# Scores two groups ahead of use, the gate in front of the squares on VectorE, and v's first loads behind z

## The chip, the cores and the metric

One core of one Trainium2 chip. The time is what the device takes for one execution, in microseconds (us). The kernel before takes 1231.67 us, the median of the 3 runs that the prediction could see (1231.24 to 1232.58). The experiments compare kernels in rounds on one chip: a ratio is the mean time of one kernel's fast runs over the mean time of the other kernel's fast runs of the same rounds, so it is not quite the ratio of the medians that stand beside it. The changed kernel was run in one round only, so an experiment is compared with it through the two ratios to the kernel before. A trace is of one run, and not always of a typical one.

In the lines of the profile, PE is TensorE's matmuls and PEld its weight loads, DVE is VectorE, ACT ScalarE, POOL GpSimd and SP SyncE; a q behind a name means the engine's queue. L282 is line 282 of the kernel in question, and the same statement has other line numbers in other kernels.

## The reference, cut to what matters

```python
# u, v: (8, 3008, 256)   z: (8, 3008, 64)   all float32
scores = (1.0 / S) * np.matmul(z, z.transpose(0, 2, 1))
attn = np.maximum(scores, 0.0) ** 2
x = u * np.matmul(attn, v)                       # the gate is this product with u
xt = x.transpose(0, 2, 1)
h = np.maximum(xt @ w_tok1, 0.0) @ w_tok2        # w_tok1 3008x256, w_tok2 256x3008
u2 = x + h.transpose(0, 2, 1)
out = u2 + np.maximum(u2 @ w_ch1, 0.0) @ w_ch2   # w_ch1 256x1536, w_ch2 1536x256
```

## The kernel before

A batch is cut into 6 blocks of 512 queries and 6 blocks of 512 keys, so it has 36 *groups* (a query block with a key block); groups are numbered n = 0 to 287 over the 8 batches. A group makes scores (TensorE), relu (ScalarE), squares (VectorE) and then 8 products with v (TensorE), 4 into each of two accumulators, one for each half of the 256 channels. In the last key block, two of the 8 (the *tail products*, one for each accumulator) have only 64 rows and come first. (The recorded texts say "block" for group where they speak of scores one or two blocks ahead.) At the end of a query block the *gate* multiplies both accumulators by u and so frees them for the next block. From batch 1 on, a squared block above the diagonal is also turned by a DMA transpose (a *flip*), which saves its mirror image, and the matmuls of the mixer of the batch before are strewn between the groups. Batch 0 has no mixer work and no flips.

```python
def scores(b, q, g):
    ...                                       # 4 matmuls (L229) into two tiles sc (tag "ps", bufs=3)
    at = sb.tile(..., tag="at", bufs=3)
    for pr, sc in enumerate(pss):
        rl = sb.tile(..., tag="rl", bufs=3)
        nc.scalar.activation(rl, sc, ACT.Relu, scale=inv_S)             # L242
        nc.vector.tensor_mul(at pair, rl, rl)                           # L246 if flipped, else L248
    if flip:
        nc.sync.dma_start_transpose(out=fl, in_=at[:])                  # L252

def gate(b, q, dh):
    nc.vector.tensor_mul(xT[:, dh], acc[dh], uT[:, :, dh])              # L308 (L313: the ragged rest)
    if dh == DT - 1:
        nc.sync.dma_start_transpose(out=x, in_=xT)                      # L317, x_sb for the mixer

def load_u(b, q): nc.gpsimd.dma_start(out=ur, in_=u rows)               # L145
def turn_u(b, q): nc.sync.dma_start_transpose(out=uT, in_=ur)           # L154

def load_w_tok2(c):                           # six parts, once per kernel
    st = sb.tile(..., tag="ws", bufs=1)       # one staging buffer
    nc.gpsimd.dma_start(out=st, in_=w_tok2 part c)                      # L171
    for h in range(DT):
        nc.gpsimd.tensor_copy(w_tok2_sb part, st)                       # L175

# what is asked for at which group (fetch[n] is issued at the head of group n)
at_group(base + q * NG + 2, lambda m=m: load_u(m // NQ, m % NQ))        # m: two blocks on
at_group(base + q * NG + 5, lambda m=m: turn_u(m // NQ, m % NQ))
at_group(base + (NQ - 1) * NG - 2 + (j if j > 1 else 0),
         lambda b=b, c=c: load_v(b + 1, c))                             # v of the next batch
at_group(NG + 1 + 4 * c, lambda c=c: load_w_tok1(c))
at_group(NG + 3 + 4 * c, lambda c=c: load_w_tok2(c))                    # groups 9, 13, ..., 29
at_group(2 * NG + 6 * part, lambda part=part: load_w_ch(part))

for n, (b, q, g) in enumerate(groups):
    for f in fetch.get(n, []): f()
    if n + 2 < NG: turn_first_z(zr0[vorder[n + 2]], zTs[0], vorder[n + 2])
    if direct_block(b, q, g): scores(*directs[ahead]); ahead += 1       # ahead starts at 1
    ...
    if not last:
        half(0); mix(n, got / 2); half(1); mix(n, 0.0)                  # half: 4 products, L282
    else:
        half(0); gate(b, q, 0); half(1); gate(b, q, 1); mix(n, 0.0)
```

`turn_first_z` turns a block of batch 0's z with four small matmuls and a copy out of PSUM by ScalarE; `double_z` makes the doubled bf16 copy that it turns; `fill(n)` issues n matmuls on zeros, to keep TensorE busy while the first data come.

## Time and profile before

| | before |
|---|---|
| time | 1231.67 us |
| span of the profiled run | 1230.7 us |
| TensorE (PE) busy | 97% |
| VectorE, ScalarE, GpSimd busy | 49%, 41%, 12% |
| waits of PE for gate, first squares, flipped squares | 12.1, 4.6, 2.0 us |

TensorE is the bound, so only what makes it start later counts. The lines that say so are in the prediction. GpSimd asks for u, v, the weights and, from batch 1 on, z.

### The profile page before, as it was taken

What the parts mean: (1) busy time and instruction counts of PE and PEld (TensorE: products, weight loads), DVE (VectorE), ACT (ScalarE), POOL (GpSimd) and SP (SyncE); (2) the same over time, 40 slices, a digit from 0 to 9 for tenths busy, and PEclk for the clock granted to TensorE, in tenths of its full rate; (3) what the DMA queues carried; (4) which work ended last, traced back from release to release, by engine and by line L of the source; (5) the groups of instructions that cost most, each with busy time, mean ns of one, the idle gap of its engine ahead of it and who ended that gap; (6) DMA issues with size and microseconds to landing.
All of it is one profiled execution on the core that took longest, in us unless ns stands there. A gap on an engine that the chain in (4) does not pass through costs nothing.

```text
span 1230.7 us, 17401 instructions
## 1 busy us (share of the span) xinstructions
PE 1198.9 (97%) x7105; PEld 626.3 (51%) x7105; DVE 603.6 (49%) x781; ACT 503.1 (41%) x525; POOL 142.5 (12%) x271
## 2 busy tenths in 40 slices
PE   7999999999999999999999999999999999999998
PEld 2334445554555445564455545455455554555566
DVE  3665654436553464435544355544544436553443
ACT  5776444343533434324434244433444334442122
POOL 2442010100101001111011111011010110000000
PEclk8999999999999999999999999999999999999999
DMA  7999966897767967669677787678866797653122
GB/s 132 147 120 146 155 134 124 136 150 134 124 140 130 159 111 141 144 116 166 118 144 131 123 145 123 131 148 129 151 122 129 132 151 129 128 106 83 33 78 67
DMA packets 436223, 157.20 MB, mean 128 GB/s; under 512 B 400112, under 2 KB 413744, under 8 KB 436144
## 3 DMA queue, kind: packets, MB, share of 16 engines
q1 hardware_dynamic: 408800, 123.78, 52.4%
q0 software_dynamic: 27344, 32.32, 19.7%
q8 instruction: 55, 0.90, 0.3%
q14 instruction: 24, 0.20, 0.0%
HBM read 65.40 MB, written 24.64 MB: 73 GB/s over the span
## 4 chain that ended last, share of the span: by engine, by line
PE 85%; DVE 7%; issue 3%; ACT 3%; DMA 1%; SPq 0%; DVEq 0%; ACTq 0%
PE acc L282 36%; PE op L389 20%; PE hp L371 18%; PE sc L229 6%; PE a_ps L336 3%; DVE xT L354 3%; ACT rl L242 2%; DVE h2pre L376 1%; DVE xT L308 1%; DVE at L248 1%; DVE at L246 1%; DMA fl<-at 1%; DMA zf<-in_z_dram 1%; PE h_ps L350 1%; ACT h2pre L378 1%
## 5 line engine op out<-in xcount | busy, mean ns | idle before, releaser
L242 ACT ACTIVATE rl<-sc 128x1024 bf16<-128x1024 f32 (+1 forms) x366 | 352.1, 1014 | 378.2 <-PE sc L229 373.0
L282 PE MATMUL acc<-at,v_sb 128*128 128x512 bf16 (+3 forms) x1464 | 359.7, 379 | 19.8 <-DVE xT L308 12.1
L282 PEld LDWEIGHTS <-v_sb 128*128 128x128 bf16 (+1 forms) x2304 | 207.8, 98 | 296.5 <-issue 100.2
L389 PE MATMUL op<-w_ch_sb,h2pre 128*128 128x256 bf16 (+1 forms) x2304 | 279.1, 273 | 0.8
L371 PE MATMUL hp<-xT,w_ch_sb 128*128 128x512 bf16 (+1 forms) x1152 | 274.8, 374 | 1.3 <-DVE xT L354 0.2
L378 ACT ACTIVATE h2pre<-hp 128x1024 bf16<-128x1024 f32 (+1 forms) x144 | 144.8, 1005 | 281.7 <-PE hp L371 280.9
L389 PEld LDWEIGHTS <-h2pre 128*128 128x128 bf16 (+1 forms) x2304 | 224.3, 98 | 62.1 <-ACT h2pre L378 6.3
L246 DVE TENSOR_TENSOR at<-rl 128x1024 bf16<-128x1024 bf16 x210 | 145.7, 695 | 191.3 <-ACT rl L242 187.7
L376 DVE TENSOR_SCALAR h2pre<-hp 128x1024 bf16<-128x1024 f32 (+1 forms) x144 | 172.5, 1199 | 78.8 <-PE hp L371 78.7
L282 PE MATMUL acc<-fl,v_sb 128*128 128x512 bf16 (+1 forms) x840 | 200.3, 370 | 0.0
L371 PEld LDWEIGHTS <-w_ch_sb 128*128 128x128 bf16 x1152 | 112.6, 98 | 131.4 <-issue 4.4
L248 DVE TENSOR_TENSOR at<-rl 128x1024 bf16<-128x1024 bf16 (+1 forms) x156 | 108.2, 702 | 94.5 <-ACT rl L242 94.3
L397 DVE TENSOR_TENSOR res<-op,u_sb 128x512 f32<-128x512 f32 x88 | 60.5, 688 | 155.7 <-PE op L389 155.7
L229 PE MATMUL sc<-zT 64*128 64x512 bf16 (+1 forms) x732 | 113.0, 381 | 2.0 <-DVE xT L354 1.0
L308 DVE TENSOR_TENSOR xT<-acc,uT 128x512 bf16<-128x512 f32 (+1 forms) x96 | 61.5, 663 | 62.8 <-PE acc L282 62.4
L145 POOL DMA_DIRECT2D ur<-in_u_dram x48 | 26.0, 542 | 434.8 <-DMA uT<-ur 434.2
L354 DVE TENSOR_TENSOR xT<-xT,h_ps 128x1024 bf16<-128x1024 bf16 (+1 forms) x48 | 53.9, 1191 | 23.0 <-PE h_ps L350 23.0
L96 POOL COPY zr<-zs 128x512 bf16<-128x512 bf16 x42 | 27.7, 660 | 311.9 <-DMA zT<-zr 311.5
L229 PEld LDWEIGHTS <-zT 64*128 64x128 bf16 x732 | 22.1, 94 | 70.6 <-issue 69.7
L350 PE MATMUL h_ps<-w_tok_sb,a_sb 128*128 128x512 bf16 (+1 forms) x192 | 43.3, 374 | 1.6 <-ACT a_sb L342 0.7
L336 PE MATMUL a_ps<-x_sb,w_tok_sb 128*128 128x256 bf16 x384 | 44.4, 273 | 0.0
L135 POOL DMA_DIRECT2D v_sb<-in_v_dram x48 | 26.0, 548 | 135.7 <-PE acc L282 135.6
(33 smaller groups left out, 157.1 us busy)
## 6 DMA issues: line engine op xcount, KB each, us to landing
out_dram<-res SPq DMA_DIRECT2D x88, 256.0 KB, 2.3
v_sb<-in_v_dram POOLq DMA_DIRECT2D x40, 256.0 KB, 4.1
ur<-in_u_dram POOLq DMA_DIRECT2D x40, 256.0 KB, 4.9
zs<-in_z_dram POOLq DMA_DIRECT2D x35, 64.0 KB, 4.9
fl<-at SPq DMA_TRANSPOSE x105, 4.4
v_sb<-in_v_dram POOLq DMA_DIRECT2D x8, 192.0 KB, 5.0
w_ch_sb<-in_moe_w_ch_dram POOLq DMA_DIRECT2D x4, 384.0 KB, 6.0
ur<-in_u_dram POOLq DMA_DIRECT2D x8, 192.0 KB, 5.6
```

Source lines behind the costliest of these rows:

```text
L229: nc.tensor.matmul(sc[:, r, :W], zT[h, k * P:(k + 1) * P], zT[h, q * QW:q * QW + W], start=True, stop=True)
L242: nc.scalar.activation(rl[:, :, :W], sc[:, :, :W], ACT.Relu, scale=inv_S)
L246: nc.vector.tensor_mul(a4[:, :, pair, :], r4, r4)
L248: nc.vector.tensor_mul(a3[:, pair, :W], rl[:, :, :W], rl[:, :, :W])
L282: nc.tensor.matmul(o, vt[rows, i, dh * P:(dh + 1) * P], rhs, start=st, stop=sp, skip_group_check=True)
L308: nc.vector.tensor_mul(xT[:, dh, :full * P].rearrange("p (t s) -> p t s", s=P), acc[:, :full * P].rearrange("p (t s) -> p t s", s=P), uT[: ...
L336: nc.tensor.matmul(st["a_ps"][:, th, :], w_tok1_sb[:, k, th * P:(th + 1) * P], x[:, :, i, :], start=(k == 0 and th == 0), stop=(k == KT - ...
L354: nc.vector.tensor_add(xT[:, :, :W], xT[:, :, :W], h[:, :, :W])
L371: nc.tensor.matmul(hp[:, r, :W], w_ch1_sb[:, dc, cc * P:(cc + 1) * P], xT[:, dc, :W], start=(dc == 0), stop=(dc == DT - 1))
L376: nc.vector.tensor_single_scalar(h2[:, :, :W], hp[:, :, :W], 0.0, AX.max)
L378: nc.scalar.activation(h2[:, :, :W], hp[:, :, :W], ACT.Relu)
L389: nc.tensor.matmul(op[:rows[i], i, :], st["h2", q, cc // 2][:, cc % 2, c0:c0 + rows[i]], w_ch2_sb[:, cc, :], start=(cc == 0 and i == 0), s ...
```

## The change

The intent is to take away three kinds of stall of TensorE: at the start (all z doublings were in front of the first squares), at block ends (the squares of the next group were in front of the gate), and in later batches (squares ready too late). Scores are made two groups ahead, so that their squares can be issued behind the gate; the first z blocks no longer share the DMA with all of v.

```diff
-    for pr, sc in enumerate(pss):            # in scores(): relu, square, relu, square
+    for sc in pss:                           # relu, relu; the squares are handed back
         rl = sb.tile(...); nc.scalar.activation(rl, sc, ACT.Relu, scale=inv_S)
-        ... squares of this pair
+        rls.append(rl)
+    def squares(): ...                       # squares, and the flip
+    return squares
 ... # start
-    for c in vorder: load_v(0, c)
+    zr0 = [double_z(zf0[c], nc.vector) for c in range(DT)]
+    for c in range(NG):
+        if DT <= c: zr0.append(double_z(zf0[c], nc.gpsimd))
+        load_v(0, c)                         # behind the doubling on GpSimd
-    fill(8) ... fill(3); scores(*directs[0]) ... fill(2);  ahead = 1
+    fill(5); turn 0; turn 1; fill(2); scores(*directs[0])(); scores(*directs[1])(); fill(3);  ahead = 2
 ... # turn_first_z: blocks 0 and 1 into acc0/acc1, copied by ScalarE; the others
+            nc.vector.tensor_copy(zT[:, c * GK:c * GK + GK, :], zp[:])
 ... # loop over groups
-        if n + 2 < NG: turn_first_z(...)     # at the head of the group
-        if direct_block(b, q, g): scores(*directs[ahead]); ahead += 1
+        if direct_block(b, q, g):
+            for _ in range(0 if n == 0 else 2 if n == NG - 2 else 1):
+                squares.append(scores(*directs[ahead])); ahead += 1
         if not last:
+            for f in squares: f()
             half(0)
+            if n + 2 < NG: turn_first_z(zr0[n + 2], zTs[0], n + 2)
             mix(n, got / 2); half(1); mix(n, 0.0)
         else:
             half(0); gate(b, q, 0); half(1); gate(b, q, 1)
+            for f in squares: f()
             mix(n, 0.0)
```

Block 0 of batch 0 now also takes its keys in the plain order 0 to 5 (`key_order`), where before the last key block came second.

## The prediction

> **What bounds the kernel now.** I read the page first, then the waits of TensorE, then the timelines of PE and DVE around three places: the start, the end of a 512-row block, the change of batch.
>
> ```profile
> PE 1198.9 (97%) x7105; PEld 626.3 (51%) x7105; DVE 603.6 (49%) x781; ACT 503.1 (41%) x525; POOL 142.5 (12%) x271
> PEclk8999999999999999999999999999999999999999
> PE 85%; DVE 7%; issue 3%; ACT 3%; DMA 1%; SPq 0%; DVEq 0%; ACTq 0%
> PE acc L282 <- DVE xT L308: 12.1, 24, 1.1
> PE acc L282 <- DVE at L248: 4.6, 1, 4.6
> PE acc L282 <- DVE at L246: 2.0, 7, 0.9
> ```
>
> TensorE is the bound, 97% busy at the full clock after the first slice, and the chain that ended last is 85% PE. No other engine passes 50%. So only time in which PE waits can be won. The waits name three kinds (us in total, times, longest): the first product of a block waits for the gate of the block before (L308, which frees the accumulator), one long wait at the start, and seven short ones for squared scores (L246). Together 18.7 us. The idle figure understates a stall, because a matmul's record includes a drain that the next normally overlaps: back-to-back matmuls start 0.23 us apart (x8 in 1.90 us), while one alone lasts 0.37. So I count a stall as the delay of a start against the regular pattern "scores 0.54 us, then products".
>
> ```profile
> 28.60 1.90 PE L282 MATMUL acc<-at,v_sb 128*128 128x512 bf16 x8
> 30.43 0.60 PE L229 MATMUL sc<-zT 64*128 64x512 bf16 x4
> 30.46 0.69 DVE L248 TENSOR_TENSOR at<-rl 128x1024 bf16<-128x1024 bf16 x1 [0.22 <-ACT rl L242]
> 31.07 1.28 DVE L308 TENSOR_TENSOR xT<-acc,uT 128x512 bf16<-128x512 f32 x2
> 31.81 0.37 PE L282 MATMUL acc<-at,v_sb 64*128 64x512 bf16 x1 [0.77 <-DVE xT L308]
> 32.41 1.77 PE L282 MATMUL acc<-at,v_sb 64*128 64x512 bf16 x7 [0.23 <-DVE xT L308]
> ```
>
> A block's end: half 0 of the products is complete near 29.7, yet the gate starts at 31.07, when the second square of the next group (30.46) is through VectorE. The next block should begin at 30.43 + 0.54 = 30.97; its first tail product starts at 31.81 (0.84 late) and the second, whose row half runs beside the first in regular groups, at 32.41. The stall is 0.84 plus (32.41 - 31.81 - 0.22 regular step) = about 1.25 us.
>
> ```profile
> 12.96 0.43 DVE L113 CAST zr<-zf 128x512 bf16<-128x512 f32 x1 [1.25 <-DMA zf<-in_z_dram]
> 13.31 1.29 DVE L248 TENSOR_TENSOR at<-rl 128x1024 bf16<-128x1024 bf16 x2
> 8.80 0.61 PE L229 MATMUL sc<-zT 64*128 64x512 bf16 x4
> 14.04 1.01 PE L282 MATMUL acc<-at,v_sb 128*128 128x512 bf16 x2 [4.64 <-DVE at L248]
> 14.04 3.57 PE L282 MATMUL acc<-at,v_sb 128*128 128x512 bf16 x8 [4.64 <-DVE at L248]
> 18.79 1.78 PE L282 MATMUL acc<-at,v_sb 64*128 64x512 bf16 x8
> ```
>
> The start: the first squares stand behind all six z doublings on VectorE, and the last doubling waits for z, which shares the DMA with all of v, until 12.96. PE idles 4.64 us, then runs its first eight products at 0.43 us each instead of 0.23.
>
> **What the Trainium skill says.** (1) "TensorE: Matmul & The Clock Gate", Part 1, What's actually happening: after an idle window of about 3.4 us the clock falls to half and comes back after about as much activity. The trace agrees: after 4.64 us idle, products at 0.43 us until 18.79. (2) "Perfetto Trace Analysis", Tensor Engine Instruction: "ACT/DVE/GPSIMD are strict FIFO", so the order in which VectorE's work is issued decides; the gate at 31.07 behind the square at 30.46 agrees. The same place says that the end of a matmul is estimated, which is why I count by starts. (3) "DMA: Bandwidth & Descriptors", Issuing engines are not separate DMA queues: transfers begun from different engines interleave on the same 16 DMA engines. The trace agrees: z from SyncE's queue landed about 1.65 us apart (casts at 9.64, 11.29, 12.96) while v was moving.
>
> **The change part by part.**
>
> Removed at the start: four of the six doublings leave VectorE for GpSimd, and because GpSimd issues the v loads after them in order, only two v loads compete with z. Working: z block 0 was doubled at 2.91; block 1 is now second in the queue, and I estimate landing at 4.2 (its issue is 0.4 us after block 0's; some v in the way). Doubling 0.43, turning about 0.5, fill(2) up to 0.86: scores at about 6.1 (5.9 before, so not sooner). First relu 0.4 + 1.03 us later, first square 0.69: data ready at 8.2. But PE now also makes the second block's scores and fill(3) first; three score buffers for four score pairs mean that the fill waits for the second relu at 8.6, and the products start at about 9.5, against 14.04: 4.5 us. If the clock stays warm through these short gaps (likely, none near 3 us), eight products save 8 x 0.21 = 1.7 us, and the turning and scores after them about 0.4. Given back: in group n = 4 two sets of scores go in a row through three buffers; the fourth pair waits for the first relu, about 0.8 us. I take 5.3 us for the start (1 us off for a chance that the clock or v is late; 3.5 to 6.5).
>
> Moved at a block's end: gate 0 no longer has squares in front, so accumulator 0 is free well before 30.97. Gate 1 can start only when half 1 is complete, at 28.60 + 1.90 = 30.50, plus a handover (a product started 0.06 us after the gate's end at 32.35): 30.57 to 31.24, so the second tail product starts at 31.30, 0.33 us late. Saved: 1.25 - 0.33 = about 0.93 us at every boundary whose next block begins with tails and has no mixer work between. In batch 0 that is 5 boundaries: 4.6 us. The change to batch 1 begins with block 0, whose half 0 needs accumulator 0 alone: whole stall of 1.2 us gone. In batches 1 to 7 only the end of block 0 has no mixer work (778 and 379 ns classes as at 278.67 and 279.26, the same shape); the other ends are covered by mixer matmuls, and I give them nothing: 7 x 0.93 = 6.5.
>
> Added by two-ahead: squares are ready a whole group (2.37 us in the regular pattern) before use. That pays for putting them behind the gates, and removes the L246 waits: six are 0.17 us idle, but the start is 0.43 late:
>
> ```profile
> 260.06 0.61 PE L229 MATMUL sc<-zT 64*128 64x512 bf16 x4
> 260.84 1.36 PE L282 MATMUL acc<-at,v_sb 64*128 64x512 bf16 x6 [0.17 <-DVE at L246]
> ```
>
> (260.84 against 260.06 + 0.54, and the second tail.) Together with what follows 0.3 to 0.4 each, 6 x 0.4 = 2.4 us.
>
> Sum before losses: 5.3 + 4.6 + 1.2 + 6.5 + 2.4 = 20.0 us. The number of matmuls in the stream is less by six only (five fillers fewer, one branch aside), so nothing is won there beyond the stalls.
>
> **The rivals.**
>
> One: the first batch runs into its transfers. Into batch 1, PE already waits for squares whose buffer is still being read by a transpose:
>
> ```profile
> 126.13 2.06 PE L282 MATMUL acc<-at,v_sb 128*128 128x512 bf16 x8 [0.93 <-DVE at L246]
> 129.80 0.37 PE L282 MATMUL acc<-at,v_sb 64*128 64x512 bf16 x1 [1.08 <-DVE xT L308]
> 115.78 14.32 SPq L252 DMA_TRANSPOSE fl<-at  x5
> 111.29 1.99 SPq L154 DMA_TRANSPOSE uT<-ur  x1
> 104.42 0.57 POOL L145 DMA_DIRECT2D ur<-in_u_dram  x1
> ```
>
> Five transposes take 2.9 us each, start only behind a transpose of u at 111.29, and that u was asked for at 104.42 by a GpSimd queue that had waited 9.5 us for weights. DMA is 96% busy from 31 to 108 us. Three score buffers in SBUF mean that squares of group m + 3 need transpose m whether scores are one or two ahead. If this chain does not move, PE arrives some 11 us early and waits: all of 5.3 + 4.6 + 1.2 and batch 1's 0.93 would be lost, leaving about 8 (1223). Against it: the chain is in part held by PE itself (SyncE waits for the gates of each block before it goes on to the turning of z, 79.23 then 80.58, and GpSimd's copy at 86.76 waits for that). I take it to move by 8 of the 11 us: 3 lost, and batch 1's own 0.9 lost with them.
>
> Two: a queue of VectorE in front of the mixer. The squares after the gate now delay the mixer's evacuations by 1.3 us where a block ends on a direct group. VectorE is 49% busy and the mixer has 3 PSUM buffers; the scores that wait for L354 (0.16 us idle, 7 times) stay. Cost 0 to 2 us.
>
> Three: all stalls vanish, the acc 1 wait too, and the start is as short as its chain: 5.3 + 1.2 for the start, 5 x 0.33 + 7 x 0.33 = 4 more: 26 us, 1206. For it speaks nothing but that my gate 1 estimate is short.
>
> Four: v comes late, because its loads now wait for z on GpSimd. v of block 2 is asked for at about 6 and needed at about 14; u of block 0 is turned before its gate at about 23 only with 1 or 2 us to spare. If this fails the gain of the start shrinks to 2 or 3.
>
> **Range and chances.** 20.0 - 3 - 0.9 = 16, so 1231.67 - 16 = 1215.5 us, 1.3% faster. The start is uncertain by 1.5, the chain into batch 1 by 3 to 5 downward, gate 1's residue by 2: 1209 to 1222.5 should hold it. Faster by over 2% needs 24.6 us, nearly every stall at once: 7%. Slower by over 2% would need a new stall in each batch, for which I see no cause: 1%.
>
> **What would show it.** First product near 9.5 us, with starts 0.22 apart; L308 waits of about 0.3 us or less instead of 0.77 + 0.23 at 12 boundaries, none at the change to batch 1; no L246 waits in batches 2 to 7; the L246 wait near 126 us not gone but longer (over 2 us), with the first batch ahead by 8 or less once it is over. Wrong would be: first product after 12, a gate wait of over 0.7 left in batches 2 to 7, a first batch that is 11 us ahead after its transposes, or new PE waits at hp or op.

Slips in the recorded text. Where it calls the stall at the end of block 0 in batches 1 to 7 "778 and 379 ns classes", it should have given the idle times 0.77 and 0.22 us of the matmuls at 278.67 and 279.26 us. "Less by six only (five fillers fewer" should be three fillers fewer (13 before, 10 after), which is six rows, each filler being a weight load and a matmul. And "three score buffers in SBUF" means the three buffers of squared scores (`at`). The terms of the start add up to 4.5 + 1.7 + 0.4 - 0.8 = 5.8, so that 5.3 takes off 0.5 and not "1 us". The 26 us of the third rival are 20.0 + 1.2 + 4 = 25.2. And "0.23 us apart" is 0.22: (1.90 - 0.37) / 7. None of these decides anything. On the clock, the products ran slow from 14.04 to 18.79, so it took some 4.7 us of work to come back, more than the 3.4 that the text calls about as much.

## More of the kernel before

The columns are: engine, tile and line, what it waited for, then us in total, times, longest us.

```profile
POOL v_sb L135 <- PE acc L282: 135.6, 24, 15.1
POOL w_tok_sb L175 <- DMA ws<-in_moe_w_tok_dram: 33.3, 6, 9.5
```

Most of GpSimd's waits are like the first line: a request for v that waits until its buffer is free, hundreds of us in sum over the run and harmless. The second line looks smaller, but it is different in kind: in `load_w_tok2` the copy stands right behind the load that it copies, so the six parts of w_tok2 hold the whole queue of requests for 33.3 us, all within the first batch.

## The result, and the profile after

| | before | after |
|---|---|---|
| time, median (lowest to highest, runs) | 1231.45 (1230.16 to 1232.58, 4) | 1224.64 (1222.73 to 1226.18, 4) |
| ratio, 95% interval | | 0.9944, 0.9927 to 0.9961 |
| span of the profiled run | 1230.7 | 1222.7 |
| mean granted clock | 0.997 | 0.997 |

The change is faster by some 7 us, within 2%. The prediction was 1215.5 us with a range of 1209 to 1222.5: it promised twice the gain, and the result is outside the range.

From the page of the changed kernel: busy time of the engines, then the shares of the chain that ended last, by engine.

```profile
PE 1191.7 (97%) x7020; PEld 624.1 (51%) x7102; DVE 606.4 (50%) x781; ACT 502.5 (41%) x521; POOL 147.1 (12%) x275
PE 81%; DMA 6%; issue 4%; DVE 4%; POOL 2%; ACT 1%; SPq 1%; DVEq 0%; POOLq 0%; ACTq 0%
```

(82 matmul records are missing from this trace: 7020 against 7102 weight loads.) VectorE's share of the chain has fallen from 7% to 4%, which was the aim, but DMA has risen from 1% to 6%, and GpSimd, which was not in the chain at all, has 2%. Something that was hidden before now sets the end. What PE waits for after the change (us in total, times, longest):

```profile
PE a_ps L349 <- DMA x_sb<-xT: 4.8, 1, 4.8
PE sc L235 <- DVE zT L129: 4.1, 4, 1.1
PE acc L295 <- DMA v_sb<-in_v_dram: 2.8, 1, 2.8
PE acc L295 <- DVE xT L321: 1.1, 2, 0.8
```

The waits for the gate fell from 12.1 us (24 times) to 1.1 us (twice), and the waits for flipped squares are gone. In their place stand four waits at the start for a copy by VectorE, and two single waits for DMA. To see what they cost, I read the *lead* of the changed kernel: the start of a given group in the trace before, minus the start of the same group in the trace after. The predicted column adds up the terms of the prediction.

| place | before | after | lead | predicted |
|---|---|---|---|---|
| batch 0, group 5, v of the last key block (28.60 / 26.95) | 28.60 | 26.95 | 1.7 | 5.3 |
| batch 1, first group | 108.26 | 99.71 | 8.5 | 11.1 |
| batch 1, its fourth group | 120.39 | 120.96 | -0.6 | |
| batch 2, first group | 258.23 | 259.68 | -1.5 | 8.1 |
| end (spans) | 1230.7 | 1222.7 | 8.0 | 16.1 |

(Group 5 has key block 5 in the changed order and key block 4 before; the count of groups is the same. 8.1 is 11.1 + 0.93 - 3 - 0.9.) So the first batch gains less than foreseen, the next stretch loses all of it, and the six batches after that gain somewhat more than was foreseen: 8.0 + 1.5 = 9.5 us from batch 2 to the end, of which 0.6 comes late in batch 7.

**The parts that worked.** PE and VectorE at the end of block 0 of batch 0, and the same ends in batch 2, in the changed kernel (start us, us, engine, line, operation, tiles, count, idle before and its releaser):

```profile
28.12 1.34 DVE L321 TENSOR_TENSOR xT<-acc,uT 128x512 bf16<-128x512 f32 x2 [0.35 <-PE acc L295]
28.66 0.60 PE L235 MATMUL sc<-zT 64*128 64x512 bf16 x4
29.11 2.18 PE L295 MATMUL acc<-at,v_sb 64*128 64x512 bf16 x8
29.38 2.53 DVE L259 TENSOR_TENSOR at<-rl 128x1024 bf16<-128x1024 bf16 x4
...
261.95 1.78 PE L295 MATMUL acc<-at,v_sb 64*128 64x512 bf16 x8
278.38 0.61 PE L235 MATMUL sc<-zT 64*128 64x512 bf16 x4
278.83 2.18 PE L295 MATMUL acc<-at,v_sb 64*128 64x512 bf16 x8
```

The gates (28.12) now run in front of the squares (29.38), and the tail products at 29.11 start 0.45 us after the scores with no wait in front. Their eight take 2.18 us, where the same eight take 1.78 at 261.95: the residue of gate 1 is 0.40 us, predicted 0.33. At 261.95 the wait for flipped squares, which stood there before, is gone.

**The start.** PE in the changed kernel:

```profile
8.62 1.02 PE L295 MATMUL acc<-at,v_sb 128*128 128x512 bf16 x4
11.59 0.60 PE L235 MATMUL sc<-zT 64*128 64x512 bf16 x4 [0.86 <-DVE zT L129]
15.34 0.60 PE L235 MATMUL sc<-zT 64*128 64x512 bf16 x4 [1.09 <-DVE zT L129]
19.09 0.61 PE L235 MATMUL sc<-zT 64*128 64x512 bf16 x4 [1.09 <-DVE zT L129]
22.84 0.82 PE L235 MATMUL sc<-zT 64*128 64x512 bf16 x6 [1.09 <-DVE zT L129]
24.35 0.39 PE L235 MATMUL sc<-zT 64*128 64x512 bf16 x2 [0.69 <-ACT rl L249]
```

and VectorE's queue beside it:

```profile
13.07 0.69 DVE L259 TENSOR_TENSOR at<-rl 128x1024 bf16<-128x1024 bf16 x1 [1.54 <-ACT rl L249]
13.99 0.69 DVE L259 TENSOR_TENSOR at<-rl 128x1024 bf16<-128x1024 bf16 x1 [0.22 <-ACT rl L249]
14.60 0.68 DVE L129 CAST zT<-zp 128x512 bf16<-128x512 f32 x1
```

The first product starts at 8.62, earlier than the predicted 9.5 and 5.4 us earlier than the 14.04 of before. But z is now copied by VectorE (L129) behind both squares of the group; the copy at 14.60 ends at 15.28, and the scores at 15.34 start right after it. Four times in a row this makes a wait of about 1.1 us, and the double set of scores in group 4 costs 0.69 more. Hence a lead of 1.7 instead of 5.3.

**The change to batch 1.** PE, changed kernel:

```profile
99.71 1.90 PE L295 MATMUL acc<-at,v_sb 128*128 128x512 bf16 x7
107.08 1.04 PE L295 MATMUL acc<-at,v_sb 128*128 128x512 bf16 x4 [2.77 <-DMA v_sb<-in_v_dram]
118.19 1.87 PE L349 MATMUL a_ps<-x_sb,w_tok_sb 128*128 128x256 bf16 x8 [4.85 <-DMA x_sb<-xT]
120.96 2.93 PE L295 MATMUL acc<-at,v_sb 128*128 128x512 bf16 x8
130.01 0.37 PE L295 MATMUL acc<-at,v_sb 64*128 64x512 bf16 x1 [0.84 <-DVE xT L321]
```

PE reaches batch 1 at 99.71, 8.5 us early, waits 2.77 us for v and 4.85 us for x_sb, and after the second wait runs eight products in 2.93 us instead of 1.90. The granted clock (third from the end in this line) shows why: it was half.

```profile
118.00:121.00 3.00, 2.81 (x13) 1.19 (x13) 0.34 (x1) 0.90 (x2) 0.32 (x1) 0.50 1.08 143
```

The eight products with x_sb (1.87 us, 1.04 just before the wait), the scores (1.03, else 0.60) and these eight lose about 2.3 us together. So the two waits and the slow clock after them, 2.77 + 4.85 + 2.3 = about 10 us, make up the whole loss; without the slow clock it would not have passed the lead that there was to lose. The chain that ended last says what lies behind it. It is followed back from the end of the run; from 10 to 120 us no step of it is on PE (start us, us, what; steps of 0.5 us or less are left out):

```profile
92.66 8.71 DMA ws<-in_moe_w_tok_dram
...
104.58 0.53 POOL v_sb L141
105.12 7.21 DMA ur<-in_u_dram
...
112.34 1.23 SPq L160
...
113.68 2.33 SPq L330
...
116.11 4.46 DMA fl<-at
```

Read it forwards: the last part of w_tok2 (ws) is in flight from 92.66; GpSimd stands at the copy of it; only then does it ask for v, and at 105.12 for u of block 1; u lands 7.21 us later, and SyncE's queue turns u (112.34), then x (113.68), then the flips (116.11). The request for u was at 104.42 in the kernel before. PE got 8.5 us faster, and this chain did not move: it is even 0.7 us later.

### The profile page after: what moved, and what is told of

Read it like the earlier page. It is cut to its first block, busy times and chain, and to the rows that moved or that the text cites. A ratio compares the mean times of both kernels' runs of the same rounds, so it can differ in the third digit from the quotient of the medians.

```text
span 1222.7 us, 17330 instructions
## 1 busy us (share of the span) xinstructions
PE 1191.7 (97%) x7020; PEld 624.1 (51%) x7102; DVE 606.4 (50%) x781; ACT 502.5 (41%) x521; POOL 147.1 (12%) x275
## 4 chain that ended last, share of the span: by engine, by line
PE 81%; DMA 6%; issue 4%; DVE 4%; POOL 2%; ACT 1%; SPq 1%; DVEq 0%; POOLq 0%; ACTq 0%
PE acc L295 33%; PE op L402 20%; PE hp L384 18%; PE sc L235 6%; PE a_ps L349 3%; DVE xT L367 2%; DMA ws<-in_moe_w_tok_dram 2%; DVE h2pre L389 1%; DMA ur<-in_u_dram 1%; DMA fl<-at 1%; DVE at L257 1%; ACT rl L249 1%; ACT h2pre L391 1%; POOL w_tok_sb L181 1%; DMA uT<-ur 1%
## 5 line engine op out<-in xcount | busy, mean ns | idle before, releaser
L295 PE MATMUL acc<-at,v_sb 128*128 128x512 bf16 (+2 forms) x1450 | 358.1, 379 | 5.0 <-DMA v_sb<-in_v_dram 2.8
L295 PE MATMUL acc<-fl,v_sb 128*128 128x512 bf16 (+1 forms) x805 | 196.1, 370 | 1.8
L321 DVE TENSOR_TENSOR xT<-acc,uT 128x512 bf16<-128x512 f32 (+1 forms) x96 | 64.1, 669 | 95.5 <-PE acc L295 94.3
L367 DVE TENSOR_TENSOR xT<-xT,h_ps 128x1024 bf16<-128x1024 bf16 (+1 forms) x48 | 53.9, 1192 | 12.8 <-PE h_ps L363 12.8
L349 PEld LDWEIGHTS <-w_tok_sb 128*128 128x128 bf16 x384 | 37.8, 99 | 12.8 <-issue 5.2
```

Of the source, the lines that this page charges most:

```text
L295: nc.tensor.matmul(o, vt[rows, i, dh * P:(dh + 1) * P], rhs, start=st, stop=sp, skip_group_check=True)
L321: nc.vector.tensor_mul(xT[:, dh, :full * P].rearrange("p (t s) -> p t s", s=P), acc[:, :full * P].rearrange("p (t s) -> p t s", s=P), uT[: ...
L349: nc.tensor.matmul(st["a_ps"][:, th, :], w_tok1_sb[:, k, th * P:(th + 1) * P], x[:, :, i, :], start=(k == 0 and th == 0), stop=(k == KT - ...
L367: nc.vector.tensor_add(xT[:, :, :W], xT[:, :, :W], h[:, :, :W])
```

## The experiments

The theory after this reading, called A: the first batch's lead is lost because the parts of w_tok2, each with its copy waiting behind its load in GpSimd's queue, hold up the requests for batch 1. The rivals: the order in SyncE's queue (E), the sheer bytes of the weights on the DMA engines, and a plain loss on TensorE. Where a text names a theory by a letter, it is a working name for the explanation told ahead of it. Times are medians in us (lowest to highest).

### Do the two parts of the reordering work alone?

`a_one_ahead`: gate in front, but scores one group ahead. `a_sq_first`: two ahead, but squares in front of the gate again.

```diff
 # a_one_ahead
-            for _ in range(0 if n == 0 else 2 if n == NG - 2 else 1):
+            for _ in range(1):
-    scores(*directs[1])()
-    ahead = 2
+    ahead = 1
 # a_sq_first
         else:
+            for f in squares: f()
             half(0); gate(b, q, 0); half(1); gate(b, q, 1)
-            for f in squares: f()
```

> The changed kernel with the gate in front but scores only one block ahead, as before. The squares that the next block needs at once then come after the gate: its first product waits for them about 1 us instead of 0.2 for the gate, and the 0.36 us per batch that two-ahead won at the second group are lost too: 6 to 9 us slower than the changed kernel, 1230 to 1234. If the gate order alone made the gain: 1224 to 1226.5.

> The changed kernel with the squares put back in front of the gate at a block's end (scores stay two blocks ahead). If the order on VectorE is what shortened the stall after block 0 of each batch, the 1.13 us there are lost again in batches 2 to 7 and nothing else: 6 to 7 us slower than the changed kernel, 1230 to 1232. If scores two ahead did it, less than 2 us slower, 1224 to 1226.5.

Measured: `a_one_ahead` 1237.21 (1235.46 to 1238.73), ratio 1.0035 (1.0 to 1.007). `a_sq_first` 1239.93 (1233.77 to 1242.79), ratio 1.0051 (1.0009 to 1.0092). Both are a little slower than the kernel before, and slower than forecast: `a_sq_first` by 8 us in the median, and its trace is of the fastest of its four runs (1233.77), so what the others lost is not known. With one group ahead the squares behind the gate come too late for the next products; PE, first block end and then the sums:

```profile
29.64 1.79 PE L295 MATMUL acc<-at,v_sb 64*128 64x512 bf16 x8 [1.45 <-DVE at L259]
```

```profile
PE acc L295 <- DVE at L257: 11.1, 13, 1.4
PE acc L295 <- DVE at L259: 9.8, 9, 2.1
```

With the squares in front again, the gate waits are back at their old size:

```profile
PE acc L295 <- DVE xT L321: 12.0, 24, 1.0
```

In batches 2 to 7 `a_sq_first` keeps 0.34 us a batch (the wait for flipped squares) and `a_one_ahead` loses 0.1 a batch, where the whole change gains 1.47. So the gate's place and the distance of two are worth something only together: the distance pays for the place.

That the two end behind the kernel before is a matter of the change to batch 1 again. They reach it with leads of only 1.6 and 1.9 us and come to batch 2 at -4.0 and -3.9, after waits of 4.4 and 5.3 us for x_sb. So the stretch can cost more than the lead: in `a_one_ahead` u was asked for only at 109.37, and in `a_sq_first` (103.89) a flip of 3.25 us stood in front of x in SyncE's queue.

### The start

`a_turn` puts the turning of z back to the head of the group and lets ScalarE copy it.

```diff
+        if n + 2 < NG: turn_first_z(zr0[n + 2], zTs[0], n + 2)   # ahead of scores
-            nc.vector.tensor_copy(zT[:, c * GK:c * GK + GK, :], zp[:])
+            nc.scalar.copy(zT[:, c * GK:c * GK + GK, :], zp[:])
```

> The changed kernel, with the turning of z in the first four groups back where it was (front of the group, copied out by ScalarE instead of VectorE). It should take away the four waits of 1.1 us of the scores for VectorE's copy. Theory A: the first batch is then 12 us ahead of the kernel before instead of 8.5, and all of it is lost at batch 1 again: time 1224 to 1225.5, the same as the changed kernel. Rival D (gains of the start reach the end): 1220 to 1221.

Measured: 1223.33 (1220.27 to 1224.78), ratio 0.9917 (0.9888 to 0.9946). PE in `a_turn`:

```profile
9.05 1.89 PE L292 MATMUL acc<-at,v_sb 128*128 128x512 bf16 x8
11.63 1.90 PE L292 MATMUL acc<-at,v_sb 128*128 128x512 bf16 x8
14.23 1.90 PE L292 MATMUL acc<-at,v_sb 128*128 128x512 bf16 x8
```

A group every 2.6 us and no wait for zT. Group 5 starts at 22.76, a lead of 28.60 - 22.76 = 5.8 us, close to the predicted 5.3, and batch 1 is reached 12.7 us early. Yet after the change of batch only 2.8 of it are left: again about 10 us are lost. In the medians, four more us at the start came to about one us at the end, and the forecast of theory A (1224 to 1225.5) was missed by little. That speaks for a chain that doesn't move with PE, but not strongly: the trace is of the fastest of the four runs (1220.27), and in it the four us are kept (2.8 at batch 2 against -1.5). There u was asked for at 100.78, 4.3 us earlier than in the changed kernel, although the first part of w_tok2 was asked for no earlier (29.38 against 29.19): the loads in between took less time. From that first request to the request for u the kernels whose w_tok2 parts stand alike took 71.4 (`a_turn`) to 79.6 us (`a_one_ahead`), 75.2 before and 75.9 after the change. The chain's own length varies by several us.

### Asking later for w_tok2

`a_late_ws` asks for parts 4 and 5 of w_tok2 at groups 34 and 36 instead of 25 and 29, so that they no longer stand in front of v and u. `b_late_ws` is the same edit on the kernel before, `a_ws_turn` the same on `a_turn`.

```diff
-        at_group(NG + 3 + 4 * c, lambda c=c: load_w_tok2(c))
+        at_group(NG + 3 + 4 * c if c < 4 else 26 + 2 * c, lambda c=c: load_w_tok2(c))
```

> The changed kernel, but the last two parts of w_tok2 (which wait one for the other on GpSimd's queue and are not needed before the second block of batch 1) are asked for after batch 1's v and u. Theory A (GpSimd's in-order queue reaches batch 1's v and u at a fixed time near 104 us, whatever TensorE does): v and u of batch 1 are asked for some 8 us earlier, the 2.8 us wait for v at 107 us goes, the 4.8 us wait for x_sb falls below 2, batch 1's second block starts 5 to 8 us earlier than in the changed kernel, time 1216 to 1219. Rival B (the flip transposes themselves are the limit, with their three buffers): the wait only moves to the squares, the second block of batch 1 is within 2 us of the changed kernel, time 1223 to 1225.

> The same edit to the kernel before. Theory A: there the first batch had no lead to lose, only the 1.26 and 1.6 us stalls near 126 and 130 us can shrink: 1229 to 1231.5. Rival C (the edit is good by itself, whatever the change): as much gain as on the changed kernel, 5 us or more, 1224 to 1226.

> Both edits. Theory A: if the late weights free the queue by more than the lead, the start's 4 us show as well: 1213 to 1216; if the queue is freed by less, the same as with the late weights alone.

Measured: `a_late_ws` 1225.91 (1223.80 to 1230.41), ratio 0.9946 (0.9913 to 0.9979): a miss, no gain over the change. `b_late_ws` 1235.35, ratio 1.0016 (0.9988 to 1.0043), not the small gain that was forecast. `a_ws_turn` 1223.86 (1219.09 to 1225.27), ratio 0.9916 (0.9878 to 0.9954), its lead going from 12.8 to -0.7. In `a_late_ws` the wait for v is gone, since u and v are asked for earlier (u at 91.39), but the wait for x_sb has grown to 7.2 us. GpSimd in `a_late_ws`:

```profile
110.70 1.20 POOL L181 COPY w_tok_sb<-ws 128x512 bf16<-128x512 bf16 x2 [12.11 <-DMA ws<-in_moe_w_tok_dram]
111.84 0.20 POOL L318 MEMSET xT<- 128x128 bf16 x1
```

The experiment made its own stall. The last block of a batch is ragged, and GpSimd clears the rest of its xT (L318) before the gate; with the copies moved to that place, the clearing, and so the gate and x_sb, wait 12.11 us for a part of w_tok2. The miss did not refute the queue; it showed the same queue holding up something else.

### The order in SyncE's queue

`a_turnu` asks for the turning of u of batch 1, block 1, four groups later, behind the transposes of x; `b_turnu` is the control on the kernel before. `best1` joins this with `a_turn` and with parts 4 and 5 of w_tok2 at groups 36 and 37.

```diff
-                at_group(base + q * NG + 5, lambda m=m: turn_u(m // NQ, m % NQ))
+                at_group(base + q * NG + (9 if m == NQ + 1 else 5), lambda m=m: turn_u(m // NQ, m % NQ))
```

> The changed kernel, but the turning of u for block 1 of batch 1 is issued four groups later. In the changed kernel that turning waited on SyncE's in-order queue for u to land at 112 us, and the turning of x for the last block of batch 0 (for which TensorE then waits 4.8 us) and six flips stood behind it. Theory E (the lead is lost in SyncE's queue behind that one turning): the 4.8 us wait for x_sb and the 0.84 us gate wait at 130 go, the 2.8 us wait for v stays; batch 1's second block is 4 to 6 us ahead of the kernel before instead of level; time 1217 to 1219.5. Theory F (bandwidth of the DMA in the first 130 us, queue order does not matter): the wait moves to another transfer, time 1223 to 1226.

> The same edit to the kernel before, as a control. Theory E: the stalls near 126 and 130 us were this queue too, 1 to 2 us gained, 1229.5 to 1231. If it gains 5 us or more, the edit is good by itself and says nothing on where the change lost its lead.

> The changed kernel with the turning of z in front of the group on ScalarE, the late turning of u, and the last two parts of w_tok2 asked for after batch 1's v and u and after the small fill of xT that the last block's turning needs. Theory E: lead of about 12.7 us at the start of batch 1 kept but for 1 to 4 us, time 1209 to 1214. Theory F: 1219 to 1224.

Measured: `a_turnu` 1221.35 (1220.31 to 1224.32), ratio 0.9909 (0.9889 to 0.9930). `b_turnu` 1231.13, ratio 0.9984 (0.9968 to 1.0000). `best1` 1223.08 (1222.07 to 1223.84), ratio 0.9922 (0.9903 to 0.9940). In the trace of `a_turnu` the wait for x_sb shrank to 2.8 us and the wait for v grew to 4.6; the lead still went from 8.2 to -1.3. In this trace the wait moved and the loss stayed, so the order on SyncE is not what causes most of it. But the median lies between the forecasts of the two theories, and the trace is of the slowest of the four runs (1224.32; the others took 1220.31 to 1221.81): that the order costs some 3 us is not excluded. `best1` missed as `a_late_ws` did, only more so:

```profile
103.97 1.89 PE L292 MATMUL acc<-at,v_sb 128*128 128x512 bf16 x4 [3.81 <-DMA v_sb<-in_v_dram]
```

```profile
113.56 1.22 POOL L178 COPY w_tok_sb<-ws 128x512 bf16<-128x512 bf16 x2 [15.73 <-DMA ws<-in_moe_w_tok_dram]
```

PE (first fence) waits 3.81 us for v even though GpSimd had asked for that batch's third v block at 85.66, and the moved copy (second fence) waits 15.73 us. In this stretch (80 to 112 us) v landed 6.5 to 20.3 us after it was asked for, in `a_late_ws` 6.7 to 14.8, and in the changed kernel 3.8 to 8.6. So asking earlier, with the rest of w_tok2 still to come, did not help: here the load on the DMA engines told as well.

### Are the weights to blame, and is it their bytes or their queue?

Four kernels give wrong results: a memset takes the place of loads. `a_no_weights` and `b_no_weights` (all weight loads of the changed kernel and of the kernel before), `a_skip_wch` (w_ch1 and w_ch2 only) and `a_skip_tok2` (w_tok2 only, with its copies). The last two take nearly the same number of elements off the DMA, 2 x 256 x 1536 = 786,432 and 256 x 3008 = 770,048; but only w_tok2 has copies that wait in GpSimd's queue.

```diff
 # a_skip_wch
-            nc.gpsimd.dma_start(out=w_ch1_sb[:, part, :], in_=moe_w_ch1[...])
+            nc.gpsimd.memset(w_ch1_sb[:, part, :], 0.01)         # and w_ch2 likewise
 # a_skip_tok2
-        st = sb.tile(...); nc.gpsimd.dma_start(out=st, ...); nc.gpsimd.tensor_copy(...)
+        nc.gpsimd.memset(w_tok2_sb[:, :, c * QW:c * QW + W], 0.01)
 # a_no_weights, b_no_weights: both of these, and w_tok1 likewise
```

> The changed kernel without the four loads of the channel weights (filled with a constant instead: the result is wrong on purpose). Takes 1.5 MB as stored, some 3 MB as read, out of the first 110 us of DMA. Theory F (bandwidth): v, u and x land earlier, both waits at the start of batch 1 shrink to under 2 us together, time 1216 to 1219. Theory E: u of block 1 is asked for at most 3 us earlier, time 1221 to 1224.

> The changed kernel with none of the weights loaded: every weight transfer of the first 110 us is replaced by a fill on GpSimd (result wrong on purpose). Theory F (the transfers of the first 110 us take their time whatever TensorE does, so TensorE's lead is turned into waits at the start of batch 1): the waits for v and x_sb there fall to under 2 us together, the lead of 7 to 9 us at the start of batch 1 is kept but for 2 or less, time 1213 to 1217. If another thing takes the lead (buffers, order), the loss of about 10 us stays: 1222 to 1225.

> The kernel before, likewise. Theory F: it was not ahead of its transfers but for the two stalls near 126 and 130 us, so 0.5 to 3 us faster than before, 1228.5 to 1231. The difference of the two is then the change with the transfers out of the way: 13 to 17 us.

> The changed kernel without w_tok2's loads and copies (a fill instead, result wrong on purpose). Theory F: as without w_ch, which is as many bytes: 1221 to 1223.5, about 5 us of the lead lost. Theory Q: nearly as without any weights: 1212.5 to 1216.

| kernel | median (lowest to highest) | ratio (95%) |
|---|---|---|
| b_no_weights | 1230.54 (1230.02 to 1231.56) | 0.9982 (0.9955 to 1.0010) |
| a_no_weights | 1212.02 (1211.85 to 1214.53) | 0.9836 (0.9807 to 0.9864) |
| a_skip_wch | 1222.52 (1220.77 to 1223.61) | 0.9914 (0.9895 to 0.9932) |
| a_skip_tok2 | 1211.90 (1211.06 to 1213.13) | 0.9832 (0.9803 to 0.9860) |

The kernel before gains nothing from losing its weight loads; it was slow enough for them to hide. The changed kernel gains about 12 us. With the weights away the change is worth 1230.54 - 1212.02 = 18.5 us instead of 7, near the 20.0 that the prediction had before it took losses off; in `a_no_weights` the lead goes from 6.6 to 8.5 over batch 1 instead of being lost. Of the two halves, w_tok2 alone brings all of it, while w_ch, the same number of elements, brings about 2 us, within the noise (its trace, of the fastest run, keeps 2.3 of a lead of 7.2, a loss of 5 instead of 10). So the bytes may matter some, and what w_tok2 has and w_ch has not, the copies in the queue, matters most.

### The queue itself, with every byte kept

`a_split_ws` is a correct kernel. The load of each part stays where it was, and only its copy is issued three groups later, so that it should find its data there. `b_split_ws` is the same edit on the kernel before.

```diff
-        at_group(NG + 3 + 4 * c, lambda c=c: load_w_tok2(c))
+        at_group(NG + 3 + 4 * c, lambda c=c: ask_w_tok2(c))      # the load
+        at_group(NG + 6 + 4 * c, lambda c=c: place_w_tok2(c))    # the copies
```

> The changed kernel, correct result, same bytes: each part of w_tok2 is asked for where it was, but its copy out of the staging buffer comes three groups later on GpSimd's queue, so the queue does not stand still for it. Theory Q (the queue): batch 1's v and u are asked for 8 us or more earlier, the loss at the start of batch 1 falls from 10 us to 4 or less, time 1215 to 1219. Theory F (load on the DMA engines): they are asked for earlier but land no earlier, time 1222 to 1226.

> The kernel before with the staging of w_tok2 split, as a control. Theory Q: it had almost no lead over its transfers, so only the stalls near 126 and 130 us (2.9 us over a regular start) can shrink: 1228.5 to 1231. If it gains 10 us or more, the split is good by itself and the change is not what it unlocks.

Measured: `a_split_ws` 1214.42 (1211.91 to 1220.19), ratio 0.9858 (0.9817 to 0.9898). `b_split_ws` 1232.08 (1231.53 to 1232.48), ratio 0.9992 (0.9959 to 1.0025). The edit is worth nothing on the kernel before and 10 us on the changed one; the intervals of the two ratios, 0.9858 here and 0.9944 for the changed kernel, are apart, though the four runs spread over 8 us (the traced one took 1212.07). The waits of GpSimd for w_tok2, changed kernel and then `a_split_ws`:

```profile
POOL w_tok_sb L181 <- DMA ws<-in_moe_w_tok_dram: 37.5, 6, 8.3
```

```profile
POOL w_tok_sb L188 <- DMA ws<-in_moe_w_tok_dram: 8.6, 2, 4.7
```

GpSimd's requests and PE at the change to batch 1, in `a_split_ws`:

```profile
88.96 0.53 POOL L141 DMA_DIRECT2D v_sb<-in_v_dram  x1 [4.54 <-PE sc L242]
91.58 0.54 POOL L151 DMA_DIRECT2D ur<-in_u_dram  x1
```

```profile
99.75 1.90 PE L302 MATMUL acc<-at,v_sb 128*128 128x512 bf16 x7
104.27 1.04 PE L302 MATMUL acc<-at,v_sb 128*128 128x512 bf16 x4
109.50 1.91 PE L356 MATMUL a_ps<-x_sb,w_tok_sb 128*128 128x256 bf16 x16
```

PE comes to batch 1 at 99.75, no earlier than in the changed kernel (99.71), so nothing was won on TensorE. But u is asked for at 91.58 instead of 105.12; GpSimd now waits for PE (4.54 us, a buffer that must come free) and in this stretch no longer for weights (the 8.6 us are at the first two parts, near 35 and 43 us), which is how it should be in a kernel bound by TensorE. PE has no wait for v or x_sb, and the chain that ended last is 90% PE. The lead goes from 8.5 to 11.0 us over batch 1.

The earlier requests also even out the DMA: with the same bytes to move, more of them move before the change of batch. Two stretches (us from the span's start) in the changed kernel and then in `a_split_ws`; after the busy times of PE, PEld, DVE, ACT and POOL come the granted clock, the busy share of the DMA engines (it can pass 1) and GB/s:

```profile
31.00:60.00 29.00, 28.78 (x143) 9.57 (x144) 20.59 (x29) 23.66 (x25) 12.98 (x21) 1.00 0.85 134
85.00:100.00 15.00, 14.89 (x83) 5.46 (x83) 11.13 (x19) 12.37 (x15) 6.89 (x12) 1.00 1.03 123
```

```profile
31.00:60.00 29.00, 28.78 (x143) 9.57 (x144) 20.53 (x29) 23.66 (x25) 16.46 (x27) 1.00 1.04 172
85.00:100.00 15.00, 14.89 (x83) 5.43 (x83) 10.45 (x19) 12.28 (x15) 5.74 (x11) 1.00 1.29 169
```

TensorE does the same in both stretches; the DMA moves 172 instead of 134 and 169 instead of 123 GB/s. Between them, from 60 to 85 us, it is about the same (132 and 136). In the first stretch the busy share of 0.85 says that the standing queue left the DMA short of work. In the second it was 1.03 at 123 GB/s, so there it was not idle but moved less; the runs do not say why.

### A version that beats both, and the order of v and z

`a_split_turn` is `a_split_ws` with the edit of `a_turn`; `a_split_turn_turnu` adds that of `a_turnu`. `a_split_v_first` is `a_split_ws` with all six v loads asked for ahead of the doublings on GpSimd, which tests the last part of the change ("v behind z").

```diff
 # a_split_v_first
+    for c in range(NG): load_v(0, c)
-    for c in range(NG):
-        if DT <= c: zr0.append(double_z(zf0[c], nc.gpsimd))
-        load_v(0, c)
+    for c in range(DT, NG): zr0.append(double_z(zf0[c], nc.gpsimd))
```

> The split staging, with the turning of z in front of the group on ScalarE as well (4 us more lead). Theory Q: 1211 to 1215. Theory F: 1220 to 1225.

> The same with the turning of u for batch 1's block 1 issued four groups later. Theory Q: 1210 to 1214; theory F: 1219 to 1224.

> The changed kernel with split staging, but all six v loads asked for ahead of the doublings of z, as in the kernel before. If v on the DMA engines delays z as it did in the kernel before (last z at 12.96 us), the third to sixth z land 3 to 5 us later, TensorE's scores wait for them in the first groups, and the time is 1 to 4 us longer than with the split alone, 1215 to 1219. If z is not delayed, the same as the split alone, 1212 to 1216.

| kernel | median (lowest to highest) | ratio (95%) |
|---|---|---|
| a_split_turn | 1213.19 (1211.58 to 1215.92) | 0.9849 (0.9812 to 0.9885) |
| a_split_turn_turnu | 1210.90 (1209.19 to 1212.42) | 0.9822 (0.9793 to 0.9852) |
| a_split_v_first | 1217.12 (1215.16 to 1222.37) | 0.9877 (0.9834 to 0.9921) |

`a_split_turn_turnu` has the lowest median of the correct kernels, 1.8% under the kernel before (its interval reaches to both sides of 2%); its distance to `a_split_turn` and `a_split_ws` lies within the noise. The repaired start brings only about 1 us over `a_split_ws`: in `a_split_turn` batch 1 is reached 12.7 us early and 11.5 are kept, where `a_split_ws` wins 2.5 over batch 1. Its trace has waits of 1.05 us for squares and 1.08 for a gate there, much as the kernel before has (0.93 and 1.08). That the chain into batch 1 binds again, only later, would explain it and is not shown. `a_split_v_first` is 2.7 us slower in the median, but the intervals overlap. In its trace the last z doubling comes at 12.83 instead of 9.75, which does not hurt the lead at batch 1 (9.2); 1.8 and 2.4 us are then lost in waits there. Whether keeping v behind z is worth anything stays open.

## Why the prediction was wrong, point by point

**Block ends: right.** Predicted 0.93 us for each boundary without mixer work; measured about 1.1 in batch 0 and 1.13 at the end of block 0 in batches 2 to 7. The residue was as foreseen (0.40 against 0.33), and the whole stall at the change to batch 1 was worth 1.1, predicted 1.2.

**Flipped squares: right.** Predicted 0.4 us in each of six batches, measured 0.34, and the waits are gone. Both terms together were to bring 8.0 us in batches 2 to 7 and brought 6 x 1.47 = 8.8. The two experiments that take one half away show that neither brings it alone.

**The start: the cause of the gain was right, the term too large by 3.6 us.** The step that failed was the sentence "Given back: in group n = 4 ... about 0.8 us". That give-back was there (0.69), but the text took the turning of z as though it stood where it had stood. The diff moved it into the middle of the group and gave its copy to VectorE, where it stands behind both squares: four waits of about 1.1 us. `a_turn`, which undoes just that, has a lead of 5.8 us at group 5.

**The first batch runs into its transfers: the mechanism was named, its size was wrong, and this is the main error.** The prediction had u's late request, saw that GpSimd "had waited 9.5 us for weights", and gave what would happen if the chain did not move: "leaving about 8 (1223)". The runs gave 8.0 us of span and 1224.64 us. So near a hit is in part luck: batches 2 to 7 and the end gave 9.5 us and not 8.0, and the change to batch 1 took 1.5 more than the lead. The failing step is "I take it to move by 8 of the 11 us". The argument for it was that SyncE and GpSimd wait for PE in places. In this stretch they do not: the request for u moved from 104.42 to 105.12, by nothing of PE's 8.5 us. The loss term, 3 us beside batch 1's own 0.9, measured 10.0 (from a lead of 8.5 to -1.5). About 2.3 of these are a cost that the text knew at the start and left out here: it counted a wait in this place by its length alone, and the clock fell to half after it.

**What holds the chain** is not in the prediction. It looked at the single wait of 9.5 us next to the late request; all six parts of w_tok2 hold the queue, 33.3 us before and 37.5 after, and what is asked for behind them comes at a time set by six loads in a row and not by PE: in the changed kernel the chain that ended last has no step on PE from 10 to 120 us. The prediction quoted the Trainium skill ("Perfetto Trace Analysis", Tensor Engine Instruction) that VectorE, ScalarE and GpSimd work off their queues strictly in order, and drew the conclusion for VectorE, and on GpSimd for v behind the doublings, but not for the six parts of w_tok2; the same sentence holds for them, as the trace shows (37.5 us), and that is where the gain went. It also foresaw the wrong wait: it named the squares near 126 us, but PE waited for v at 107.08 and for x_sb at 118.19. That GpSimd's queue is the cause was shown by `a_split_ws` (same bytes, copies later, 10 us won back, nothing on the kernel before), and `a_skip_tok2` against `a_skip_wch` agrees.

**The other rivals.** No new waits of a size at the mixer's evacuations appeared (one of 0.2 us at hp, as before), so rival two cost next to nothing. Rival four, late v at the start, did not happen.

**What stays open.** How much of the loss comes from the late request itself and how much from the DMA being crowded when the late requests come in a bunch: `a_late_ws` and `best1` asked earlier and won nothing, but made stalls of their own and found v slow to land, `a_skip_wch` halved the loss in its trace by taking bytes away, and `a_split_ws` changes both at once. And the variants of the changed kernel spread over 2 to 9 us from run to run, where the kernel before, but for single runs near 1235 to 1238, spreads over 2 to 4; no run says why. The mean granted clock does not: all four runs of `a_split_ws` show 0.999. The varying length of GpSimd's chain, 71.4 to 79.6 us, is a candidate.

## What to carry to other kernels

Before you count a gain, ask of every chain that the faster engine will meet whether it is held by that engine or runs on a clock of its own: follow the request back in the queue of the engine that issues it, and treat a gain that ends in such a chain as lost until that queue is shown to move. Count a long wait by more than its length: here 4.85 us of waiting cost about 2.3 more, since the clock was half after it. An engine that issues loads should not wait for one of them: put a copy that needs a load's data several steps behind the load. And when a diff moves a piece of work to another engine, look up what now stands in front of it there.

## What the Trainium skill lacked or had wrong

- "DMA: Bandwidth & Descriptors", section Issuing engines are not separate DMA queues: it says that starting DMAs from several engines only saves the sequencer's time for starting them, usually small. True of the start itself (a request took GpSimd 0.5 to 0.9 us here), but the section lacks that whatever else waits in the issuing engine's queue delays the requests behind it (the page's list of rules does say to issue a DMA early and to wait on its semaphore late, but for the sake of the setup cost): GpSimd stood 37.5 us at copies of just-loaded weights, and issuing those copies three groups later took the kernel from 1224.64 to 1214.42 us with the same bytes.
- "TensorE: Matmul & The Clock Gate", section Back-to-back issue gap: it gives about 131 ns for each matmul of 512 columns in a sustained stream and calls the formula that gives about 216 ns too high. Here eight such matmuls with their weight loads take 1.90 us, the last lasting 0.37, so they start (1.90 - 0.37) / 7 = 0.219 us apart, in a stream at full clock: here the formula holds, and the sustained figure does not.
